# A third factoring level across pairs of octs in a dilated causal convolution, with bank sums by DVE adds and the first ten tiles by the plain tap sum

## The chip, the core and the metric

The kernel runs on one core of one Trainium2 chip. The time is the device time of one execution in microseconds (us), quoted as the median of several executions. A program on one core has no second die to compare with, so "fast" in the run lists means within 1.5% of the fastest run of the same kernel; all runs quoted here are fast. Engines: PE is TensorE (matmuls), PEld its weight loads, DVE is VectorE, ACT is ScalarE, POOL is GpSimd, SP is SyncE, whose queue issues most of the loads here. "ACTq" and "SPq" are the instruction queues of ACT and SP when they issue transfers. In this kernel every matmul writes into one tensor of eight "banks" (0 to 7) in PSUM; all other tiles lie in SBUF. The "granted clock" is the share of full speed at which TensorE ran.

## The reference

```python
# x (2, 16000, 144), w (15, 144, 288), w_o (144, 144), all bf16; dil = 2, K = 15
xp = jnp.pad(x, ((0, 0), (28, 0), (0, 0)))
h = sum over i of einsum('btc,cd->btd', xp[:, 28 - 2*i : 28 - 2*i + T, :], w[i])
f, g = h[..., :144], h[..., 144:]
z = jnp.tanh(f) * _sigmoid(g)
return z @ w_o
```

The 32000 rows are cut into 128 segments of 250 consecutive steps, one segment per partition. "Tile" k holds step k of all segments: 128 rows. Dilation 2 means that tile k needs tiles k, k-2, ..., k-28, so even and odd tiles never meet. Eight consecutive tiles are an "oct": four tiles of each parity. There are 31 octs and 2 tiles ahead of them (called oct -1).

A channel vector of 144 is 128 + 16. The 16 left-over channels of eight taps are packed into one 128-row operand (XB), so a plain tap sum costs 15 + 2 = 17 matmuls of 288 columns per tile.

## The kernel before

A fast-FIR factoring in two levels works on the four tiles of one parity in one oct (a "quad", with parity r). It needs nine short sub-filters, fed with sums of weights (WC, WS) and differences of inputs (VE, VF, DU, DE, DF, BE, BF), instead of 16 pieces of the plain sum: 41 matmuls for four tiles instead of 68.

```python
        def S1(n):                       # 4 matmuls, then a copy of the bank
            o, r = quads[n]
            b = take()
            a = b + 1
            g.add("pe", region(a, [(lambda o_=o - i: XA[:, aslot(o_), r, :]) for i in range(4)], [wc(0, i) for i in range(4)], True), ...)
            g.add("act", lambda e: e.activation(bank(b), bank(a), ACT.Copy), r=[("bank", a)], w=[("bank", b)], dur=0.43)
        # ... S2: VE x 4 into bank a, ACT copies it to U, VF x 4 into bank b, DVE makes DD = bank b - U
        # ... S3: DU x 4 + XB into a and into b, DVE makes two new banks: a + DD, b - DD
        # ... S4: DE / DF / BE / BF products, 19 matmuls, into the four banks; tanh and gate of each pair
```

Per oct: 82 convolution matmuls of 288 columns, then a projection by w_o (11 matmuls of up to 288 columns), for which a transposing load turns z around. All operations are entered into a graph. On the host, a model of the engines (with assumed durations) decides the order in which each engine issues them. That order is then fixed: on the chip an engine waits at its next instruction even if a later one is ready.

```python
SEM_LAT = 0.07
DMA_LAT = 1.9
DMA_RATE = 200e3
MM = 0.12
# ...
            if op.dma:
                free[op.eng] = st + op.dur
                t0 = max(dma_free, st + op.dur)
                dma_free = t0 + op.nbytes / DMA_RATE
                op.end = dma_free + DMA_LAT
```

The inputs of an oct are first copied by DVE into a staging buffer, then loaded, transposed, by SP. There are two staging buffers of each kind, so the copy for oct o waits for the load of oct o-2:

```python
        def load_xb(o):
            s, q = bslot(o), o % NST     # NST = 2
            # ...
            g.add("dve", cp, r=sorted(ck, key=str), w=[("STB", q)], dur=0.36)
            g.add("sp", lambda e: e.dma_start_transpose(XB[:, s, :, :], STB[:, q, :, :].rearrange("p a b -> p (a b)")),
                  r=[("STB", q)], w=[("XB", s)], dur=1.3, dma="xb", nbytes=8 * 128 * 128 * 2)
```

Transfers take turns on a few semaphores. Where there are fewer semaphores than transfers, an issue waits until the earlier transfer on the same semaphore has landed. The raw weights WA come in four pieces, issued by ACT, on three semaphores (`"wa": 3`).

## Time and profile before

| | before |
|---|---|
| median | 379.54 us (379.22 to 380.3, 4 runs) |
| span of the profiled execution | 377.9 us |
| convolution matmuls | 31 x 82 + 34 = 2576 |
| steady state, one oct | 11.03 us |

The page of the kernel before: busy time of each engine with its share of the span, the row of the granted TensorE clock in 40 slices, and the chain of waits by engine.

```profile
PE 364.5 (96%) x3067; PEld 290.3 (77%) x3067; DVE 242.2 (64%) x642; ACT 174.2 (46%) x361; POOL 15.0 (4%) x30
PEclk9999999999999999999999999999999999999996
PE 91%; DVE 5%; DMA 1%; ACT 1%; ACTq 1%; issue 0%
```

The chain of waits follows the work back from the last instruction, at each step to what it had waited for. It is 91% PE: TensorE bounds this kernel. The busy share alone wouldn't have told it. The Trainium skill ("Perfetto Trace Analysis", section "Identifying the Most-Contended Engine") warns that the busy share of matmuls is a poor measure of how close a kernel is to its limit, because matmuls are pipelined. This case agrees, if weakly: PE shows 96% before and after the change, though by the count explained in the result it lost 18.8 us of 378 (5.0%) before and 23.9 us of 369 (6.5%) after.

The chain of waits of the kernel before in one stretch of the steady state (start, length, engine and line):

```profile
223.93 0.25 PE PS L653 x3
224.18 9.55 PE PS L555 x78
233.74 0.74 PE PS L653 x8
234.48 0.49 PE PS L555 x4
234.97 0.25 PE PS L653 x3
```

L555 is a convolution matmul and L653 a projection. One oct is 78 + 4 convolution and 11 projection matmuls, and repeats after 234.97 - 223.93 = 11.04 us. A convolution matmul takes 9.55 / 78 = 0.1224 us. The Trainium skill ("TensorE: Matmul & The Clock Gate", section "Wait — 56ns, not 53.3ns?") gives columns / 2.4 GHz + about 2.5 ns, 122.5 ns for 288 columns, and the trace agrees. So PE has no slack in the steady state; only fewer matmuls can shorten it.

The table by windows of the kernel before (window, length, then busy us and count of PE, PEld, DVE, ACT, POOL, then the clock, the DMA share and GB/s):

```profile
0.00:40.00 40.00, 29.93 (x267) 23.46 (x268) 26.59 (x81) 12.90 (x26) 15.04 (x30) 0.96 0.86 210
40.00:70.00 30.00, 30.00 (x253) 24.11 (x251) 26.24 (x73) 13.12 (x28) 0.00 (x0) 1.00 0.93 206
100.00:200.00 100.00, 100.00 (x845) 80.38 (x844) 67.03 (x175) 48.33 (x100) 0.00 (x0) 1.00 0.58 123
```

PE is full from 40 us on. DVE (67%) and ACT (48%) have room. The start is the weak part: waits of PE there, in the table of PE waits of the kernel before (line that waited, what it waited for: us in total, times, longest):

```profile
PE PS L555 <- DVE DD L689: 2.4, 1, 2.4
PE PS L555 <- DVE XA L419: 2.2, 1, 2.2
```

Together they are 4.6 us in which PE waited for DVE: for the difference DD of two banks (L689) and for an evacuation of transposed x (L419). Both lie in the first 40 us.

### The profile page before, as it was taken

The page shows a single profiled execution, that of the slowest core. Times are in us where ns is not written, and L with a number is a line of the kernel's source. Part 1 is how long each engine was busy: PE and PEld are TensorE (multiplying, and loading weights), DVE is VectorE, ACT ScalarE, POOL GpSimd, SP SyncE. Part 2 cuts the span into 40 slices and gives each one's busy share as a digit, 9 for nine tenths or more (in the row PEclk, how much of TensorE's full clock was granted, in tenths as well). Part 3 has the DMA queues.
Part 4 walks back from the last instruction along what each step waited for, and adds up shares of the span by engine and source line. Part 5 has one row for each costly group of instructions (what it writes and reads, how often), then busy time and mean ns, then how long its engine had stood idle before and what let it go on. Part 6 is the DMA issues. An engine that isn't in the chain of part 4 may idle for free.

```text
span 377.9 us, 7552 instructions
## 1 busy us (share of the span) xinstructions
PE 364.5 (96%) x3067; PEld 290.3 (77%) x3067; DVE 242.2 (64%) x642; ACT 174.2 (46%) x361; POOL 15.0 (4%) x30
## 2 busy tenths in 40 slices
PE   8668999999999999999999999999999999999996
PEld 7445788887888788888788888878888888888873
DVE  1897889777676766677666666766665665553341
ACT  1522454454544445444444544444454444445443
POOL 5820000000000000000000000000000000000000
PEclk9999999999999999999999999999999999999996
DMA  8589969995586644844755356456335434211221
GB/s 224 122 264 243 259 91 264 169 213 134 114 157 182 120 89 93 212 88 94 117 119 94 88 117 88 94 116 121 91 88 120 87 65 91 63 51 44 64 46 49
DMA packets 111647, 46.73 MB, mean 124 GB/s; under 512 B 103598, under 2 KB 106079, under 8 KB 110845
## 3 DMA queue, kind: packets, MB, share of 16 engines
q1 hardware_dynamic: 108858, 44.67, 54.2%
q10 hardware_dynamic: 2243, 1.25, 1.3%
q8 instruction: 24, 0.39, 0.5%
q0 software_dynamic: 512, 0.33, 0.4%
q14 instruction: 10, 0.08, 0.1%
HBM read 11.82 MB, written 9.22 MB: 56 GB/s over the span
## 4 chain that ended last, share of the span: by engine, by line
PE 91%; DVE 5%; DMA 1%; ACT 1%; ACTq 1%; issue 0%
PE PS L555 81%; PE PS L653 8%; DMA WA<-in_w_dram 1%; DVE WC L452 1%; DVE VE L501 1%; PE PS L618 0%; PE PS L620 0%; DVE VF L501 0%; DVE DU L501 0%; DVE DE L501 0%; ACTq L353 0%; DVE STA L472 0%; PE PS L609 0%; DVE WS L452 0%; PE PS L608 0%
## 5 line engine op out<-in xcount | busy, mean ns | idle before, releaser
L584 ACT ACTIVATE TS<-PS 128x576 bf16<-128x576 f32 x125 | 81.5, 652 | 102.1 <-PE PS L555 101.9
L588 DVE SCALAR_TENSOR_TENSOR Z<-TS 128x288 bf16<-128x288 bf16 x125 | 56.9, 455 | 46.6 <-ACT TS L584 46.2
L555 PE MATMUL PS<-WA,DE 128*128 128x288 bf16 x496 | 81.6, 287 | 0.8 <-DVE PS L700 0.8
L555 PE MATMUL PS<-WS,DU 128*128 128x288 bf16 x434 | 71.0, 286 | 2.4 <-DVE DD L689 2.4
L555 PE MATMUL PS<-WA,DF 128*128 128x288 bf16 x434 | 71.2, 286 | 0.2 <-DVE PS L703 0.2
L686 ACT ACTIVATE U<-PS 128x288 f32<-128x288 f32 x62 | 25.5, 411 | 72.6 <-PE PS L555 72.5
L555 PEld LDWEIGHTS PS<-WA,DE 128*128 128x128 bf16 x496 | 47.8, 98 | 13.1 <-DVE PS L700 1.1
L555 PEld LDWEIGHTS PS<-WS,DU 128*128 128x128 bf16 x434 | 42.3, 98 | 13.3 <-DVE DD L689 2.7
L555 PEld LDWEIGHTS PS<-WA,DF 128*128 128x128 bf16 x434 | 42.2, 98 | 11.2 <-DVE PS L703 0.6
L689 DVE TENSOR_TENSOR DD<-PS,U 128x288 f32<-128x288 f32 x62 | 28.3, 457 | 30.6 <-PE PS L555 20.6
L658 ACT ACTIVATE OS<-PS 128x432 bf16<-128x432 f32 (+1 forms) x91 | 41.2, 488 | 13.9 <-PE PS L653 13.6
L555 PE MATMUL PS<-WC,VE 128*128 128x288 bf16 x248 | 41.0, 289 | 0.7 <-ACT PS L676 0.5
L555 PE MATMUL PS<-WC,XA 128*128 128x288 bf16 x248 | 40.5, 286 | 0.4 <-DVE WC L452 0.4
L653 PE MATMUL PS<-WOR,ZT 128*128 128x144 bf16 (+1 forms) x333 | 39.8, 253 | 0.0
L555 PE MATMUL PS<-WB,XB 128*128 128x288 bf16 x128 | 36.2, 286 | 0.0
L555 PE MATMUL PS<-WB,BE 128*128 128x288 bf16 x124 | 35.6, 287 | 0.0
L555 PE MATMUL PS<-WB,BF 128*128 128x288 bf16 x124 | 35.5, 286 | 0.0
L501 DVE TENSOR_TENSOR BF<-XB 128x512 bf16<-128x512 bf16 x31 | 13.1, 423 | 34.1 <-PE PS L555 34.1
L555 PE MATMUL PS<-WC,VF 128*128 128x288 bf16 x186 | 33.3, 289 | 0.0
L653 PEld LDWEIGHTS PS<-WOR,ZT 128*128 128x128 bf16 x333 | 27.8, 98 | 5.8
L703 DVE TENSOR_TENSOR PS<-PS,DD 128x288 f32<-128x288 f32 x62 | 28.6, 462 | 5.2 <-PE PS L555 0.9
L555 PEld LDWEIGHTS PS<-WC,VE 128*128 128x128 bf16 x248 | 24.1, 98 | 7.3 <-ACT PS L676 0.8
(71 smaller groups left out, 366.0 us busy)
## 6 DMA issues: line engine op xcount, KB each, us to landing
out_dram<-OS SPq DMA_DIRECT2D x30, 288.0 KB, 2.2
Xr<-in_x_dram SPq DMA_DIRECT2D x6, 1152.0 KB, 6.2
WA<-in_w_dram ACTq DMA_DIRECT2D x3, 288.0 KB, 7.2
Xr<-in_x_dram SPq DMA_DIRECT2D x1, 864.0 KB, 4.5
Xr<-in_x_dram SPq DMA_DIRECT2D x2, 288.0 KB, 5.2
Xr<-in_x_dram SPq DMA_DIRECT2D x1, 576.0 KB, 4.5
Xp<-in_x_dram SPq DMA_DIRECT2D x2, 252.0 KB, 5.4
XA<-STA SPq DMA_TRANSPOSE x31, 3.3
```

What stands on the lines that cost most here:

```text
L452: g.add(eng, lambda v: v.tensor_tensor(dst(), a(), b(), ALU.add), r=r, w=wk, dur=dur)
L501: return g.add("dve", lambda v: v.tensor_tensor(dst(), a(), b(), ALU.subtract), r=r, w=wk, dur=dur)
L555: return lambda t: t.matmul(bank(b), lhsT=lhs(), rhs=rhs(), start=start, stop=True, skip_group_check=True)
L584: return a.activation(TS[:, s, :, :], src, ACT.Tanh)
L588: return v.scalar_tensor_tensor(dst, TS[:, s, :, D:N2], 1.0, TS[:, s, :, 0:D], ALU.add, ALU.mult)
L653: return t.matmul(PS[:, c0:c0 + n * D], lhsT=ZT[:, zt, blk_, :], rhs=WOR[:, wi_:wi_ + n, :].rearrange("p a b -> p (a b)"), start=first, st ...
L658: return a_.activation(OS[:, os_, a0:c0, :].rearrange("p e d -> p (e d)"), PS[:, bo * 512:bo * 512 + (c0 - a0) * D], ACT.Copy, scale=0.5)
L686: g.add("act", lambda e: e.activation(U[:, u, :], bank(a), ACT.Copy), r=[("bank", a)], w=[("U", u)], dur=0.43)
L689: g.add("dve", lambda v: v.tensor_tensor(DD[:, u, :], bank(b), U[:, u, :], ALU.subtract), r=[("bank", b), ("U", u)], w=[("DD", u)], dur=0.48)
L703: g.add("dve", lambda v: v.tensor_tensor(bank(e), bank(b), DD[:, u, :], ALU.subtract), r=[("bank", b), ("DD", u)], w=[("bank", e)], dur=0.48)
```

## The change

Its intent: fewer matmuls in the steady state, and a start in which PE has useful work while DVE makes the weight sums and differences.

- Two successive octs (30 octs make 15 pairs) share three of the nine sub-filters. For such a sub-filter, two octs need 2 common products and 2 difference products each, instead of 4 each: 6 instead of 8. A "unit" is one parity of one pair, 8 tiles: 76 matmuls (2x2 XC, 2x6 XR, 2 SC, 2x2 SR, 2x8 EF, 2x19 DD) instead of 82.
- The sums of banks that put the sub-filters together are four DVE adds per half unit, PSUM + SBUF into PSUM. ACT copies more banks: bank 7 to 6, p to q, p to p+1, and both X banks to SBUF (UX).
- Oct 0 and the two tiles of oct -1 (10 tiles) go by the plain tap sum: 170 matmuls, which need only transposed x and raw weights.
- The projections are no longer placed where they fit; they stand in PE's main order and use banks 6 and 7 by turns.
- The host's model is new: other durations, a latency per engine, priorities; `DMA_RATE` 300e3 instead of 200e3. `DMA_LAT` stays 1.9 us.

```diff
-SEM_LAT = 0.07
+SEM_LAT = 0.05
 DMA_LAT = 1.9
-DMA_RATE = 200e3
-MM = 0.12
+DMA_RATE = 300e3
+MM = 0.122
+LAT = {"pe": 0.17, "act": 0.12, "dve": 0.08, "pool": 0.1, "sp": 0.0}
 # ... the scheduler uses LAT and a priority
+        def common(b, t0, t1, i0, keys):
+            g.add("pe", [mm(b, t0, lambda: WT[:, i0, :], True), mm(b, t1, lambda: WT[:, i0 + 1, :], False)], ...)
+        def XC(u, k):          # 2 products common to both octs, bank 7, ACT copies it to bank 6
+        def XR(u, k):          # 2 + 1 products for each oct into banks 7 and 6, ACT takes both to UX
+        def SC(u):             # 2 common products into bank p, ACT copies p to q
+        def SR(u, h):          # 2 products for oct h, ACT copies p to p+1
+        def EF(u, h):
+            # ... 4 VE products into p, 4 VF products into p + 1
+            for dst, src, k in ((n, p, 0), (n + 1, p + 1, 0), (p, p, 1), (p + 1, p + 1, 1)):
+                g.add("dve", lambda v, dst=dst, src=src, k=k: v.tensor_tensor(bank(dst), bank(src), UX[:, k, us, h, :], ALU.add), ..., prio=0)
+        # ... DD: the 19 products of S4, as before
+        for u in range(NUN):
+            def slot(b):
+                if todo:
+                    project(*todo.pop(0), b)
+            EF(u, 0)
+            slot(6)
+            # ... XC, DD, XR of this and the next unit
+            if u == NUN - 1:
+                ship_pair(o1, 6, -2, BANK_O)
+                ship_pair(o1, 2, -2, BANK_O)
+                store_some(o1, [2, 6], 2, 4, 0)
+            slot(7)
+            EF(u, 1)
+            slot(6)
+            # ...
```

`ship_pair` is the way out of the last oct: PE transposes z, DVE and ACT evacuate, PE projects, ACT evacuates. It stood in the kernel before too; new is that its two early calls stand in front of `slot(7)`, `EF(u, 1)` and `slot(6)`. `slot(b)` places the next waiting projection, in bank b, so these projections use the same banks 6 and 7 as the early calls.

> **What bounds it now.** TensorE. The chain of waits is 91% PE, 81% of it convolution matmuls. In steady state it repeats every 11.03 us per oct (8 output tiles): 82 matmuls of 288 columns in 10.04 us, 122.4 ns each, plus 11 projection matmuls in 0.99 us. The Trainium skill ("TensorE: Matmul & The Clock Gate", section "Wait — 56ns, not 53.3ns?") gives columns/2.4 GHz + 2.5 ns back to back, 122.5 ns here: the trace agrees. The table by windows shows PE 100% busy from 40 to 370 us, DVE 67%, ACT 48%. In the first 40 us PE does roughly 12 us of useful work; the chain runs through DVE from 10.9 to 26 us (weight sums, differences), and in part until 37. The tail after the last convolution matmul is 8.8 us.
>
> **PE work.** For 8 tiles 82 matmuls become 76: each of three shared sub-filters takes 2 common + 2x2 difference products for two octs instead of 8. 30 units: 180 less. Oct 0 goes by plain tap sum: 10 tiles x 17 = 170 matmuls instead of 34 + 82 = 116, 54 more. Net -126 x 0.1224 = **-15.4 us**. Projections are unchanged.
>
> **The start.** Plain tap sums need only transposed x and raw weights, so PE works 20.8 us (170 x 0.1224) while DVE makes sums and differences. Before, tap sums began at 15.1 us; I expect 13 to 15.5, ending at 34 to 36. DVE has about 24 us of work (0.34 us per difference back to back, 0.31 to 0.38 per sum) from 11 us on, done near 35. The first unit then pays a serial run matmul, ACT copy, matmul, evacuation: 3 us. PE's steady run starts near 38 us with oct 0 done; before, oct 0 was in its last phase at 37. Worth another 5 to 8 us.
>
> **DVE and ACT.** Per 8 tiles DVE does 8 PSUM adds (0.37 us apart) instead of 6, plus 0.5 us of second-level differences: 8.3 to 9 us of 10.3, over 80%. ACT does five copies (0.41) and two double evacuations (0.65) instead of four copies: 7.3 of 10.3, 71%. Neither becomes the bound, but both now stand in short loops: matmul, copy of bank 7 to 6, matmul, evacuation, with the projection sharing those banks; and matmuls, four adds, matmuls. Timing one unit by hand leaves slack of 0.2 to 0.5 us at most steps, nearly none where the shared bank's copy must precede the next products. I allow 0.1 us per unit, 3 us in all; it could be 10.
>
> **Sum** (span): 36 (start) + 3 (first unit) + 30 x 76 x 0.1224 = 279.1 + 30 x 0.99 = 29.7 + 3 (stalls) + about 8 (tail) = 358.8; time was 1.8 us above the span: **360 us**, range 354 to 368. Faster by over 2% (below 372): 0.92; within: 0.06; slower: 0.02.
>
> **What would show it.** In the chain, an oct pair every 20.6 us (22.06 before); convolution matmuls about 2450; PE nearly 100% busy from 40 us on; PE waits for ACT copies or DVE adds under 5 us; tap sums filling 14 to 35 us with no DVE chain there; DVE over 80%, ACT near 70%. If the pair takes over 21.3 us, the short loops stall PE and the gain halves; the table of PE waits will name adds or copies.
>
> **What would make it wrong.** In-order DVE at 80% load delaying adds behind differences; the projection's eviction holding banks 6 and 7; a first unit waiting for the transposing loads of octs 1 and 2, now issued only after the weights have landed.

## The result, and the profile after

| | before | after |
|---|---|---|
| median | 379.54 us (379.22 to 380.3, 4 runs) | 370.02 us (369.66 to 371.04, 4 runs) |
| ratio after / before | | 0.9751, 95% interval 0.9726 to 0.9775 |
| span of the profiled execution | 377.9 us | 369.3 us |
| convolution matmuls | 2576 | 2450 |
| steady state, 8 tiles | 11.03 us | 10.30 us |

A ratio is the mean time of one kernel's fast runs over that of the other's fast runs of the same rounds, so it isn't quite the ratio of the medians. The kernel is faster by 2.5%, as the direction said, but 370 us lies above the predicted 354 to 368 us.

The page of the kernel after, the same three lines, and the chain by line:

```profile
PE 353.4 (96%) x2971; PEld 279.7 (76%) x2971; DVE 266.6 (72%) x729; ACT 225.4 (61%) x449; POOL 18.5 (5%) x30
PEclk9999999999999999999999999999999999999978
PE 78%; DMA 11%; DVE 7%; ACT 1%; SPq 1%; issue 1%; ACTq 1%
PE PS L588 69%; PE PS L690 7%; DMA XB<-STB 7%; DMA WA<-in_w_dram 2%; DMA Xr<-in_x_dram 1%; DVE STB L506 1%; DMA XA<-STA 1%; DVE Z L621 1%; DVE WC L468 1%; SPq L508 1%; DVE PS L767 1%; DVE VE L517 0%; DVE BF L517 0%; PE PS L651 0%; ACTq L366 0%
```

The chain was 91% PE and is now 78% PE: 11% of the span is spent in loads, 7% of it in the transposing load of XB. The clock row has two slices below 9 at its end.

The chain of waits of the kernel after in the steady state:

```profile
84.59 5.02 PE PS L588 x41
89.61 0.37 PE PS L690 x4
89.98 3.31 PE PS L588 x27
93.29 0.37 PE PS L690 x4
93.66 0.98 PE PS L588 x8
94.64 0.25 PE PS L690 x3
94.89 5.02 PE PS L588 x41
```

41 + 27 + 8 = 76 convolution and 11 projection matmuls in 94.89 - 84.59 = 10.30 us for 8 tiles, 20.60 for a pair of octs. That is the predicted number exactly. The table by windows of the kernel after:

```profile
0.00:40.00 40.00, 34.69 (x330) 28.81 (x330) 25.73 (x82) 10.92 (x21) 18.46 (x30) 0.96 0.89 204
40.00:70.00 30.00, 25.17 (x203) 18.95 (x204) 26.79 (x76) 16.54 (x35) 0.00 (x0) 1.00 1.05 225
100.00:200.00 100.00, 99.45 (x840) 79.32 (x839) 80.57 (x221) 67.58 (x134) 0.00 (x0) 1.00 0.64 135
```

In the steady state all is as predicted: PE 99%, DVE 81%, ACT 68%. PE does more in the first 40 us (34.69 us busy instead of 29.93). But from 40 to 70 us PE is busy 25.17 us of 30, and before it was full there. So the missing gain isn't in the steady state. It is in the first pairs and at the ends.

To put sizes to this, I counted the time that PE lost: for each two successive matmuls of the trace, the distance of their starts less columns / 2.4 GHz + 2.5 ns. Half clock counts as lost. This is my sum over the trace's records, not a view of the profile.

| stretch | lost before | lost after |
|---|---|---|
| 0 to 39.3 us (after: until the last tap sum) | 14.1 | 8.0 |
| 39.3 to 70 us | 0 | 6.0 |
| 70 to 349 us | 0 | 1.7 |
| 349 us to the last matmul | 4.7 (all after 363) | 8.2 |
| all | 18.8 | 23.9 |

The start gained 6.1 us and gave 6.0 of it back in the first pairs. The end lost 3.5 us more than before. What is left is the smaller PE work: the span less the lost time fell from 359.1 to 345.4 us, by 13.7 us. The prediction had 15.4 us for the convolution matmuls alone; the new start also has 16 more transposes and 16 more warm-up matmuls of 128 columns, an estimated 1.8 us by the same formula (32 x 0.056), less two of 288 columns.

**The first pairs.** The table of PE waits of the kernel after:

```profile
PE PS L588 <- DVE PS L767: 4.4, 5, 1.4
```

L767 are the DVE adds of banks. PE waited for them only five times in 60 half units, up to 1.4 us each, and the three longest of these lie before 70 us (at 46.77, 53.38 and 63.94 us). It isn't a little in every unit. Why were the adds late? The timeline of DVE in the kernel after, around the second of these waits (start, length, engine, line, operation, tiles, shape, count, then in brackets the idle time before it and what ended it):

```profile
49.89 0.43 DVE L506 COPY STB<-XBc 128x1024 bf16<-128x1024 bf16 x1 [1.26 <-DMA XB<-STB]
...
51.25 0.43 DVE L488 COPY STA<-Xr 128x1024 bf16<-128x1024 bf16 x1 [0.22 <-DMA XA<-STA]
...
52.86 1.55 DVE L767 TENSOR_TENSOR PS<-PS,UX 128x288 f32<-128x288 f32 x4
```

and the timeline of PE in the same kernel:

```profile
51.56 0.41 PE L588 MATMUL PS<-WT,DU 128*128 128x288 bf16 x2
53.38 0.66 PE L588 MATMUL PS<-WA,DE 128*128 128x288 bf16 x4 [1.41 <-DVE PS L767]
```

DVE stood idle for 1.26 us at the copy into a staging buffer whose earlier load hadn't landed, and 0.22 us at the next. The adds stood behind these copies in DVE's order and were late by about as much as PE waited: 1.41 us. Before the first of the three waits DVE had stood 3.3 us for loads, 2.08 us of it at one staging copy at 28.06 us; before the third, 0.89 us. The Trainium skill ("Perfetto Trace Analysis", section "Tensor Engine Instruction (MATMUL, LD_WEIGHTS)") calls DVE and ACT strict first-in, first-out; the trace agrees: DVE idles at the copy and runs nothing from behind it.

The chain of waits of the kernel after shows the same loads in its first part:

```profile
21.80 6.23 DMA XB<-STB
...
47.84 3.38 DMA XA<-STA
...
57.80 4.93 DMA XB<-STB
```

The host's model gives such a transposing load 1.9 us + 262144 bytes / 300e3 = 2.8 us. In these lines it took 3.4 to 6.2 us; all those issued in the first 40 us of this trace took 2.5 to 6.2 us, 4.3 us in the median. The Trainium skill ("DMA: Bandwidth & Descriptors", section "Anatomy of one DMA — SWDGE (gpsimd) path") fits 2.0 us + bytes / 436e3 to transfers issued by GpSimd, 2.6 us for this size as an estimate: these loads, issued by SP among many others, are slower than that, and the measured times decide.

**The start.** The timeline of ACT in the kernel after:

```profile
2.75 6.56 ACTq L356 DMA_DIRECT2D WA<-in_w_dram  x2
...
11.00 1.02 ACT L423 ACTIVATE XA<-PS 128x1024 bf16<-128x1024 bf16 x1 [8.09 <-issue]
```

ACT is held 6.56 us at the issue of weight pieces: the fourth must wait for the semaphore of the first. Only at 11.00 us does ACT evacuate its first transposed x, and the first tap sum starts at 16.58 us.

**The end.** The timeline of PE in the kernel after, inside the last unit:

```profile
352.47 0.23 PE L651 MATMUL PS<-WOR,ZTL 128*128 128x144 bf16 x1 [0.47 <-ACT ZTL L645]
...
353.70 0.23 PE L641 MATMUL PS<-ID,Z 128*128 128x128 bf16 x1 [0.50 <-ACT OS L656]
...
356.36 0.90 PE L690 MATMUL PS<-WOR,ZT 128*128 128x144 bf16 x4 [0.50 <-ACT OS L656]
357.05 1.17 PE L588 MATMUL PS<-WC,VE 128*128 128x288 bf16 x4
```

Two `ship_pair` calls one after the other, each a chain PE, ACT, PE, ACT, through the banks that the next projection in PE's order needs. PE must wait for all of it. Four waits of about 0.5 us (the third of them, at 354.88, is left out above) are 1.9 us; but the four products at 357.05 then show 1.17 us, where a group of four has 0.65 us elsewhere. The table by windows of the kernel after, around it:

```profile
351.30:354.90 3.60, 2.15 (x15) 1.04 (x12) 1.20 (x4) 1.69 (x4) 0.00 (x0) 0.98 0.30 56
356.40:361.60 5.20, 5.20 (x24) 3.43 (x25) 1.66 (x4) 0.94 (x2) 0.00 (x0) 0.50 0.24 75
```

The granted clock is 0.50 for that stretch; the trace's clock records put it at half from 354.78 to 361.61 us. The Trainium skill ("TensorE: Matmul & The Clock Gate", section "What's actually happening") speaks of a free-running window of 3413 ns and of half clock after an idle window. The length agrees: 6.83 us is two windows, and in four other profiles (after_again, wa_sem4, ring4, lat4) the clock is at half for one, 3.41 us, at this place. But the window before the fall wasn't idle: PE was busy 2.15 us of 3.60, and no wait was over 0.50 us. The same page (section "A second HAM failure mode: psum-queue depth-cycling") does tell of many short idles between groups of matmuls that bring the clock down; that is nearer to what is seen here.

### The profile page after: what moved, and what is told of

Same layout as the page of the kernel before. It is cut to its first block, busy times and chain, and to the rows that moved or that the text cites. A ratio compares the mean times of both kernels' runs of the same rounds, so it can differ in the third digit from the quotient of the medians.

```text
span 369.3 us, 7518 instructions
## 1 busy us (share of the span) xinstructions
PE 353.4 (96%) x2971; PEld 279.7 (76%) x2971; DVE 266.6 (72%) x729; ACT 225.4 (61%) x449; POOL 18.5 (5%) x30
## 4 chain that ended last, share of the span: by engine, by line
PE 78%; DMA 11%; DVE 7%; ACT 1%; SPq 1%; issue 1%; ACTq 1%
PE PS L588 69%; PE PS L690 7%; DMA XB<-STB 7%; DMA WA<-in_w_dram 2%; DMA Xr<-in_x_dram 1%; DVE STB L506 1%; DMA XA<-STA 1%; DVE Z L621 1%; DVE WC L468 1%; SPq L508 1%; DVE PS L767 1%; DVE VE L517 0%; DVE BF L517 0%; PE PS L651 0%; ACTq L366 0%
## 5 line engine op out<-in xcount | busy, mean ns | idle before, releaser
L767 DVE TENSOR_TENSOR PS<-PS,UX 128x288 f32<-128x288 f32 x240 | 94.4, 458 | 4.2 <-PE PS L588 4.0
L588 PE MATMUL PS<-WA,DE 128*128 128x288 bf16 x480 | 79.0, 288 | 4.5 <-DVE PS L767 4.4
L694 ACT ACTIVATE OS<-PS 128x432 bf16<-128x432 f32 (+1 forms) x91 | 44.3, 488 | 36.8 <-PE PS L690 36.8
L716 ACT ACTIVATE PS<-PS 128x288 f32<-128x288 f32 x150 | 59.3, 397 | 9.7 <-PE PS L588 7.0
L690 PE MATMUL PS<-WOR,ZT 128*128 128x144 bf16 (+1 forms) x333 | 45.2, 256 | 0.5 <-ACT OS L656 0.5
L588 PE MATMUL PS<-WS,GU 128*128 128x288 bf16 x210 | 44.1, 286 | 0.7 <-ACT PS L716 0.7
L737 ACT ACTIVATE UX<-PS 128x576 f32<-128x576 f32 x60 | 38.9, 648 | 3.9 <-PE PS L588 1.4
L588 PEld LDWEIGHTS PS<-WS,GU 128*128 128x128 bf16 x210 | 20.5, 98 | 6.4 <-ACT PS L716 1.2
L588 PE MATMUL PS<-WT,DU 128*128 128x288 bf16 x120 | 24.5, 286 | 0.7 <-ACT UX L737 0.7
L588 PE MATMUL PS<-WC,GX 128*128 128x288 bf16 x120 | 24.3, 286 | 0.0
```

The lines of the kernel that those rows point to most:

```text
L588: return lambda t: t.matmul(bank(b), lhsT=lhs(), rhs=rhs(), start=start, stop=True, skip_group_check=True)
L690: return t.matmul(PS[:, c0:c0 + n * D], lhsT=ZT[:, zt, blk_, :], rhs=WOR[:, wi_:wi_ + n, :].rearrange("p a b -> p (a b)"), start=first, st ...
L694: g.add("act", lambda e: e.activation(OS[:, os_, a:c, :].rearrange("p e d -> p (e d)"), PS[:, bo * 512:bo * 512 + (c - a) * D], ACT.Copy, ...
L716: g.add("act", lambda e: e.activation(bank(c), bank(b), ACT.Copy), r=[("bank", b)], w=[("bank", c)], dur=0.29, prio=prio)
L737: return e.activation(UX[:, k, u % NU, :, :], src, ACT.Copy)
L767: g.add("dve", lambda v, dst=dst, src=src, k=k: v.tensor_tensor(bank(dst), bank(src), UX[:, k, us, h, :], ALU.add), r=[("bank", src), ("UX ...
```

## The experiments

The theory: the change does what it should in the steady state, and the prediction's miss is three separate things, each at a place of its own: (a) the two output pairs in PE's order in the last unit, with the half clock they bring on; (b) ACT's queue held by a missing semaphore in the start; (c) DVE adds in the first pairs, behind copies that wait for loads, because the order was made with too short a load latency.

Rivals: the end is only the clock, or only the waits; (c) is a shortage of staging buffers, not a wrong order; the short loops of copies and adds stall PE in every unit; and the whole gain is the better model of the scheduler, not the factoring.

All kernels of this section give the right result. Times are medians of four executions, five for the last one; every call had its own runs of the kernel before on the same chip (medians 378.78, 377.80, 379.63 and 378.15 us in the four calls). tail_moved, tail_warm, wa_sem4 and ring4 ran together; then after_again, ringAB, best1 and best2; then lat4, best3 and before_sched; then best5. They are told here by what they test.

### tail_moved: the two output pairs later in PE's order, through another bank

```diff
-            if u == NUN - 1:
-                ship_pair(o1, 6, -2, BANK_O)
-                ship_pair(o1, 2, -2, BANK_O)
-                store_some(o1, [2, 6], 2, 4, 0)
             slot(7)
             EF(u, 1)
             slot(6)
+            if u == NUN - 1:
+                ship_pair(o1, 6, -2, UB[u][0])
+                ship_pair(o1, 2, -2, UB[u][0])
+                store_some(o1, [2, 6], 2, 4, 0)
```

> The changed kernel with the last oct's two early output pairs moved behind the second half of the last unit, and their transposes put into a bank pair that is free by then, so that no projection waits for them. Theory (order of banks 6 and 7 stalls PE, and the idle lowers the granted clock): the 5.95 us lost on PE from 350 to 360 us and most of the 2.3 us after it go, the granted clock stays near full until the last few us, and the time falls from 370 by 4.5 to 6.5 us. Rival (this tail is work and latency that any order pays: the output transposes, copies and stores of the last oct): the time stays within 1.5 us of 370.

Measured: 364.06 us (363.11 to 366.25), ratio to before 0.9620 (0.9575 to 0.9665). This interval lies below that of the unedited kernel in the repeat further down (0.9678 to 0.9774). From 349 us to the last matmul PE lost 3.7 us instead of 8.2, and from the start of the last unit to the last instruction it took 17.4 us instead of 21.9. The clock didn't fall in this stretch, and the first four products of `EF(u, 1)` took 0.65 us instead of 1.17, in PE's timeline of tail_moved:

```profile
351.40 0.65 PE L588 MATMUL PS<-WC,VE 128*128 128x288 bf16 x4
```

So the waits and the half clock both came from the pairs as they stood. This is (a). The edit changed the place of the pairs and the banks of their transposes together; whether one of the two would have been enough wasn't tested.

### tail_warm: keep the waits, give PE dummy work in them

```diff
             if u == NUN - 1:
                 ship_pair(o1, 6, -2, BANK_O)
                 ship_pair(o1, 2, -2, BANK_O)
                 store_some(o1, [2, 6], 2, 4, 0)
+                for _ in range(22):
+                    g.add("pe", lambda t: t.matmul(PS[:, UB[u][0] * 512:UB[u][0] * 512 + N2], lhsT=ID[:], rhs=WARM[:], start=True, stop=True, skip_group_check=True),
+                          r=["ID", "WARM"], w=[("bank", UB[u][0])], dur=MM)
```

> The changed kernel with 22 dummy matmuls put between the steps of the stalled tail, so that PE waits as before but is not idle. It prices the clock part alone. If the lower granted clock after the stall costs what the matmul spacing says (240 instead of 122 ns for some 22 matmuls), the time falls by 1.5 to 3 us, while the waits for the output copies keep their place; if the clock is not lowered by this idle, the time stays or rises by up to 0.5 us.

Measured: 367.73 us (366.29 to 369.85), ratio 0.9713 (0.9667 to 0.9759). This interval overlaps that of the unedited kernel (0.9678 to 0.9774 in the repeat below), so the times alone don't decide it. The traces do: from the start of the last unit to the end 19.9 us instead of 21.9 (20.7 in the repeat), and the group of four at full speed again, in PE's timeline of tail_warm:

```profile
356.10 0.65 PE L588 MATMUL PS<-WC,VE 128*128 128x288 bf16 x4
```

Idling for the pairs thus has two costs: the waits themselves and the half clock behind them. All profiles of this study bear this out. In the six with the pairs in their old place and no dummy matmuls the clock fell to half in the last unit: twice for 6.83 us (after, ringAB: 21.9 and 21.7 us from the start of the last unit to the end) and four times for 3.41 us (20.6 to 20.8 us). tail_warm has no such fall (19.9 us), nor have the five with the pairs moved (17.4 to 17.6 us). So the half clock cost 0.7 to 2.0 us and the waits 2.3 to 2.6 us. Neither rival ("only the clock", "only the waits") holds.

### wa_sem4: one more semaphore for the weight pieces

```diff
-        g.assign(mksem, {"xp": 8, "wa": 3, "wb": 2, "xr": NX, "xa": 4, "xb": 6, "zt": 3, "st": 4, "wor": 16})
+        g.assign(mksem, {"xp": 8, "wa": 4, "wb": 2, "xr": NX, "xa": 4, "xb": 6, "zt": 3, "st": 4, "wor": 16})
```

> The changed kernel with four instead of three semaphores for the four weight loads, so that the ACT queue no longer waits for the first load to land before it issues the last one; same order on every engine. Theory (ACT begins its evacuations at 11.0 us because its queue is held by that wait): ACT starts by about 8.5 to 9.5 us, the first tap-sum matmul moves from 16.6 to about 14 to 15.5 us, the end of the tap sums moves with it, and the time falls by 1 to 2.5 us. Rival (the landing of the weights and of x sets the start): first tap-sum matmul within 0.5 us of 16.6 and the time within 0.7 us of 370.

Measured: 366.41 us (365.24 to 368.57), ratio 0.9693 (0.9646 to 0.9740); again the intervals overlap, and the trace decides. ACT's timeline in wa_sem4:

```profile
2.76 1.10 ACTq L356 DMA_DIRECT2D WA<-in_w_dram  x2
...
7.48 1.02 ACT L423 ACTIVATE XA<-PS 128x1024 bf16<-128x1024 bf16 x1 [4.56 <-PE PS L415]
```

The issue takes 1.10 us instead of 6.56, ACT starts at 7.48 us instead of 11.00, and what it waited for until then was PE's transposes, its real input. Tap sums begin at 13.63 us, a little earlier than expected, and the first unit at 34.71 us (39.33 without the edit). Over all profiles of this study, tap sums begin at 15.2 to 17.0 us in the seven profiles of the new kernel without this edit (17.0 us in after_again) and at 13.5 to 13.9 us in the five with it. This is (b). Of the 4.6 us at the end of the tap sums 2.9 are the earlier beginning; the other 1.7 are the half clock from 16.86 us on, which wa_sem4 doesn't have. None of the five profiles with this edit has it in the tap sums, and five of the seven without it do; why isn't shown. The first EF starts at 40.44 us instead of 43.93: part of the 4.6 us is lost again, because PE now waits 1.8 us for DVE's differences across the two octs (GU) in the first unit. The waits for adds are still there, 3.0 us in all.

### ring4: four staging buffers for STB, with the order kept

```diff
-    NST = 2
+    NST, NSB = 2, 4
-        STB = sb("STB", [NP, NST, 8, 128], BF16)
+        STB = sb("STB", [NP, NSB, 8, 128], BF16)
 # ... in load_xb; ring_dma[o] is the load of oct o
-            s, q = bslot(o), o % NST
+            s, q = bslot(o), o % NSB
-            g.add("dve", cp, r=sorted(ck, key=str), w=[("STB", q)], dur=0.34)
+            cop = g.add("dve", cp, r=sorted(ck, key=str), w=[("STB", q)], dur=0.34); held.append((cop, ring_dma.get(o - 2)))
 # ...
-        _ms = g.schedule()
+        held = [(c, d) for c, d in held if d is not None and d not in c.deps]; [c.deps.add(d) for c, d in held]; g.schedule(); [c.deps.discard(d) for c, d in held]
```

The copy's old dependence on the load of oct o-2 is put back while the host makes the order and dropped after it, so that the order is the same on every engine and only the wait is gone; the copy still waits for the load of oct o-4 from its own slot.

> The changed kernel with four instead of two staging buffers in front of the transposing loads of the narrow channel block; same order on every engine, only that wait is gone. Theory (in-order DVE stands behind a staging copy that waits for a transposing load of two octs before, and the adds that PE needs stand behind it): the 5.8 us that DVE waits for that load go, the PE waits for the adds fall from 4.4 to under 1.5 us, and the time falls by 2.5 to 4.5 us. Rival (DVE simply has too much to do in the first pair, waits or not): the PE waits for the adds stay above 3 us and the time within 1 us of 370.

Measured: 366.54 us (365.84 to 368.57), ratio 0.9686 (0.9645 to 0.9727). PE's waits and DVE's waits in the kernel ring4 (two answers, PE first):

```profile
PE PS L588 <- DVE PS L767: 2.7, 2, 1.4
```

```profile
DVE STA L488 <- DMA XA<-STA: 4.1, 7, 1.8
```

This interval, too, overlaps that of the unedited kernel. Behind the second of PE's waits for adds, up to 300 us, the loss went from 2.7 us (1.7 in the repeat) to 0.6 us. But the first two waits stayed, and DVE now waits at the other kind of copy, STA, for 4.1 us (0.7 before). The expectation held in part: DVE's waits for the narrow block's loads are gone, but PE's waits for adds fell only to 2.7 us, not under 1.5.

### after_again and ringAB: the repeat, and four staging buffers of both kinds

after_again is the kernel after, unedited, so that the second call has its own reference. ringAB gives STA four slots too, with the same order on every engine. The two extra slots of each kind lie in Xp, a buffer of x that is dead by then; their copies wait for its last readers.

```diff
-    NST = 2
+    NST, NSB = 2, 4
 # ... in load_xa and load_xb: o % NSB; slots 2 and 3 are in Xp
-            s, q = aslot(o), o % NST
+            s, q = aslot(o), o % NSB
 # ... dependences on the load of oct o-2 held for the order only, as in ring4
```

> The changed kernel unchanged, on the same chip as the next ones, to compare them on one chip: 0.975 of the kernel before. The spread of its start is of interest: if the landing of the first weights varies from run to run, the first tap-sum matmul will not be at 16.6 us again, but between 15 and 17.

> The changed kernel with four staging buffers for both transposing loads (two of each in the space of the x block that only the start uses); same order on every engine. ring4, with four for the narrow block only, took away all losses after 60 us but left two waits for adds of 1.5 us near 43 and 50 us. Theory (those two are the same thing on the wide block: DVE waited 1.8 us at 49 for a staging buffer of it): the wait at 50 us goes, waits for adds fall to under 1.8 us in all, and the time is 0.5 to 2 us below ring4's ratio of 0.9686. Rival (in the first pair DVE is simply behind with the preparations, which stand before the adds in its order): both waits stay at over 1 us each and the time equals ring4's.

Measured: after_again 368.26 us (366.20 to 369.17), ratio 0.9726 (0.9678 to 0.9774); ringAB 366.09 us (365.99 to 366.78), ratio 0.9675 (0.9636 to 0.9714). In ringAB nothing is lost after 70 us, but PE still waits 2.5 us for adds in the first pairs. DVE's waits in ringAB:

```profile
DVE XBc L386 <- DMA Xr<-in_x_dram: 3.9, 2, 2.5
```

With no staging buffer to wait for, DVE waits at the next thing in its order, the chunk of x itself. The expectation was missed, and the time equals ring4's within the intervals, as the rival said. That spoke against "too few buffers" as the cause of the first waits: here buffers more moved the wait to the next load in the order.

### lat4: the load latency of the host's model, alone

```diff
-DMA_LAT = 1.9
+DMA_LAT = 4.0
```

Two staging buffers as in the change; only the order in which the engines issue differs. PE's order is the same; DVE's and that of the loads on SP are not, and on ACT one evacuation moves. One clause of the expectation, on the latency of early loads, is cut, because the traces don't show its range; what the trace of the change shows is stated above (2.5 to 6.2 us).

> The changed kernel with one constant of the host's scheduling model changed: the latency that it takes for a load, 4.0 instead of 1.9 us (the traces show 3.3 us for a transposing load[...]). PE's order stays, DVE's static order changes: copies that wait for loads move behind other work. Theory (the adds stand behind waiting copies because the model that made the order takes loads to be faster than they are): DVE's waits for loads fall from about 6 us to under 3, PE's waits for adds from 3 to 4.4 us to under 2, ratio 0.965 to 0.970 against 0.9726 to 0.9751 of the changed kernel. Rival (only the number of buffers matters): the waits and the time stay, 0.972 to 0.976.

Measured: 365.50 us (363.41 to 366.79), ratio 0.9642 (0.9618 to 0.9666), below the interval of after_again (on another chip, each against the kernel before on its own). The table of PE waits no longer names the adds, and DVE's waits for loads are 0.4 us in all. PE's timeline in lat4, at the place shown above:

```profile
48.33 0.41 PE L588 MATMUL PS<-WT,DU 128*128 128x288 bf16 x2
48.57 0.65 PE L588 MATMUL PS<-WA,DE 128*128 128x288 bf16 x4
```

The 1.41 us in front of the second group are gone. From the end of its tap sums (37.8 us) to 340 us PE lost 2.6 us, where the change unedited lost 7.5 us from 39.3 to 340, and 5.8 us in the repeat; 1.4 of the 2.6 are the serial first unit. This is (c): the cause was the order, made for loads of 2.8 us (whether DVE's or that of the loads on SP isn't separated). With another order two buffers were enough, while four buffers in the old order left the first waits.

### before_sched: the kernel before with only the new model of the scheduler

```diff
-SEM_LAT = 0.07
+SEM_LAT = 0.05
-DMA_RATE = 200e3
-MM = 0.12
+DMA_RATE = 300e3
+MM = 0.122
+LAT = {"pe": 0.17, "act": 0.12, "dve": 0.08, "pool": 0.1, "sp": 0.0}
 # ... and the priorities and durations of the change
```

> The kernel before with the other half of the change alone: the new host model (latencies, priorities, durations) without the third level, the plain tap sums and the new buffers. Theory (the gain is fewer matmuls): PE was already dense from 40 us on, so at most the 14 us lost in the first 40 us can move; ratio 0.990 to 1.005. Rival (a good part of the change's 2.5% is better scheduling): 0.985 or below.

Measured: 382.56 us (382.38 to 384.34), ratio to before 1.0090 (1.0064 to 1.0117). The new model alone makes the old kernel slower by 0.9%, a little beyond the expected 0.990 to 1.005. So the gain is the factoring and the start by tap sums, with the order of work that goes with them, and the rival falls. Neither of the two was run without the other; their shares come from the count above alone (13.7 us less PE work; 6.1 us won in the start, of which 6.0 were lost again).

### best1, best2, best3: mends put together, with the larger staging rings

best1 is tail_moved + wa_sem4 + ringAB. best2 is best1 with the differences DU of both octs, and the second-level differences made from them, ahead of the others in DVE's preparation. best3 is tail_moved + wa_sem4 + lat4 with the larger rings known to the model.

```diff
 # best2, against best1
         def prepare(m):
-            prep(2 * m + 1)
-            prep(2 * m + 2)
+            v_second(2 * m + 1)
+            v_second(2 * m + 2)
+            for o in (2 * m + 1, 2 * m + 2):
+                v_first(o)
+                v_third(o)
+                b_diffs(o)
 # best3, against best1
-DMA_LAT = 1.9
+DMA_LAT = 4.0
 # ... and no dependences held for the order: the model sees four slots
```

> The three mends together: tail pairs moved, four weight semaphores, four staging buffers of both kinds. If the three are independent losses, their gains add: about 5 + 2 to 3 + 2.5 us, ratio 0.945 to 0.952 of the kernel before, which is 358 to 361 us at this kernel's 379 and what the prediction said of the change. If they hide one another (an earlier start only makes DVE wait for its loads), 0.955 to 0.96.

> best1 with the preparation of a pair in another order: the second-level differences, which the first matmuls of a pair need, before the others. In all runs so far PE waited 0.8 to 1.9 us for them in front of the first unit. Expected: that wait under 0.5 us, time 0.5 to 1.5 us below best1; if DVE's total work up to the first adds is the limit, the wait only moves to the adds and the time is that of best1 within 0.7 us.

> best1 (0.9565) with the same constant, and with the model told of the four buffers. In best1 PE lost 2.2 us at 40.6 us and then ran at a low clock until 46, behind a copy that waited for a chunk of x. Expected: that loss under 1 us, 1 to 3 us less than best1, ratio 0.949 to 0.954. If the load itself is the limit (its issue comes late on the queue), it stays at 0.956.

Measured: best1 361.78 us (361.18 to 362.89), ratio 0.9565 (0.9528 to 0.9603); best2 362.32 us (361.88 to 363.01), ratio 0.9578 (0.9543 to 0.9613); best3 366.30 us (365.96 to 366.93), ratio 0.9653 (0.9635 to 0.9672). All three missed the gain that was hoped for. best1 and best2 fell where the alternative in their expectations had put them (0.955 to 0.96; within 0.7 us of best1); best3 was worse than both branches of its expectation.

In best1 DVE reached the chunk of x early and stood there, ahead of the adds. The timeline of DVE in best1:

```profile
38.77 0.23 DVE L386 COPY XBc<-Xr 128x256 bf16<-128x256 bf16 x1 [1.73 <-DMA Xr<-in_x_dram]
```

PE then waited 2.2 us in all for adds, and the clock records show half clock from 43.5 to 46.9 us after it. In best2 PE waited for adds 3.9 us in all, 2.8 us at the longest: the wait only moved. In best3, PE's waits name something new:

```profile
PE PS L690 <- DMA ZT<-Z: 5.5, 2, 2.7
```

With large rings in the model, copies and loads are issued far ahead, and the transposing load of z, which the projection needs, stands behind them in SP's queue. So a larger ring with a good latency was worse than a small ring with a good latency. That the loads issued early cause this wait is argued from their order in the queue; best5, with small rings, tests it.

### best5: the three mends with the two staging buffers of the change

```diff
-DMA_LAT = 1.9
+DMA_LAT = 4.0
 # ... the two output pairs moved as in tail_moved
-        g.assign(mksem, {"xp": 8, "wa": 3, ...})
+        g.assign(mksem, {"xp": 8, "wa": 4, ...})
```

> The changed kernel with three mends: tail pairs moved, four weight semaphores, load latency of 4.0 us in the model, and the two staging buffers as they were. best3 waited 5.5 us for the transposing load of the output, which stood on the load queue behind the loads that four buffers let it issue early; lat4, with two buffers, waited 0.4 us for it. If that is the reason, the gains of the three mends add: about 1.2% (tail) + 0.5% (weights) + 0.9% (model) below the changed kernel's 0.974, ratio 0.944 to 0.951, and the wait for the output's load stays under 1 us. If an earlier start alone brings it back, ratio 0.955 or above.

Measured: 358.40 us (357.53 to 359.99, five runs), ratio to before 0.9491 (0.9466 to 0.9516). The expectation (0.944 to 0.951) held: PE's waits for the load of z are 0.8 us in all. best5 is faster than both kernels. Its page:

```profile
PE 348.4 (98%) x2971; PEld 277.8 (78%) x2971; DVE 266.2 (75%) x729; ACT 226.0 (64%) x449; POOL 18.1 (5%) x30
PEclk9999999999999999999999999999999999999999
PE 89%; DMA 4%; DVE 3%; ACT 2%; SPq 1%; issue 0%
```

The table by windows of best5, at the place where the change had 25.17:

```profile
40.00:70.00 30.00, 29.33 (x245) 22.94 (x243) 28.11 (x80) 19.26 (x38) 0.00 (x0) 1.00 1.03 219
```

The chain is 89% PE again, the clock is full until 1 us before the end, and PE is busy 29.33 us of 30 from 40 to 70 us with no wait for adds. PE lost 10.4 us in all: 4.8 in the first 39.3 us, 1.6 from there to 340 us, and 3.9 at the end.

| kernel | edit | median us | ratio to before, with interval | place of the effect |
|---|---|---|---|---|
| after_again | none | 368.26 | 0.9726 (0.9678 to 0.9774) | |
| tail_moved | pairs later | 364.06 | 0.9620 (0.9575 to 0.9665) | end |
| tail_warm | dummy matmuls | 367.73 | 0.9713 (0.9667 to 0.9759) | end, clock only |
| wa_sem4 | 4 semaphores | 366.41 | 0.9693 (0.9646 to 0.9740) | start |
| ring4 | 4 STB buffers | 366.54 | 0.9686 (0.9645 to 0.9727) | waits after the first two |
| ringAB | 4 + 4 buffers | 366.09 | 0.9675 (0.9636 to 0.9714) | the wait moves on |
| lat4 | latency 4.0 us in the model | 365.50 | 0.9642 (0.9618 to 0.9666) | first pairs |
| before_sched | new model, old kernel | 382.56 | 1.0090 (1.0064 to 1.0117) | |
| best5 | three mends | 358.40 | 0.9491 (0.9466 to 0.9516) | all three |

## Why the prediction was right or wrong

The prediction was a sum for the span. Its terms against the traces of the change and of best5:

| term | predicted | after | best5 |
|---|---|---|---|
| tap sums end | 36 | 39.3 | 34.6 |
| PE work of 30 units (279.1 + 29.7) | 308.8 | 309.1 | 308.8 taken |
| first unit, and stalls of all units | 3 + 3 | 7.7 | 4.5 |
| lost inside the last unit | 0 | 6.7 | in the line above |
| after the last convolution matmul | 8 | 6.5 | 7.9 |
| span | 358.8 | 369.3 | 355.8 |

For the change, the PE work is 362.85 (end of the last convolution matmul) - 39.3 less 7.7 + 6.7 lost. For best5 the predicted work is taken as given, and the 4.5 us are what remains of 347.9 - 34.6; they hold the early output pairs, too.

- **What bounds it, and the steady state: right.** A pair of octs in 20.6 us was predicted and measured; convolution matmuls about 2450, measured 2450; DVE over 80%, measured 80.6%; ACT near 70%, measured 67.6%. The short loops of copies and adds hardly stall PE in the steady state (1.7 us from 70 to 349 us). The waits for adds and ACT copies, which were to stay under 5 us, were 5.8 us (4.4 and 1.4), most of them before 70 us.
- **"an oct pair every 20.6 us ... PE nearly 100% busy from 40 us on": the second half is wrong.** PE was busy 25.17 us of the 30 from 40 us on.
- **"The start": the step failed by 3.3 us.** "I expect 13 to 15.5, ending at 34 to 36": it was 16.58 and 39.3. The prediction took ACT's evacuations of x for granted and didn't see that ACT's queue is held by the fourth weight piece (wa_sem4 began at 13.63 us). The rest, 1.7 us, is clock: in the profiled run it was at half from 16.86 to 20.28 us, so that the first 90 matmuls of the tap sums took 12.7 us instead of 11.0. Its "roughly 12 us of useful work" in the first 40 us of the kernel before was too low as well: the trace has 138 convolution matmuls there, an estimated 16.9 us at 0.1224.
- **"I allow 0.1 us per unit, 3 us in all": wrong in kind and in place.** With 3 us for the first unit, the term was 6 us and measured 7.7, so the size was off by little. But it isn't a little in each unit: 6.0 of the 7.7 us lie before 70 us, and from there to 349 us the units lost 1.7 us together. Among what would make it wrong, the prediction named "In-order DVE at 80% load delaying adds behind differences" and "a first unit waiting for the transposing loads". Both happened, joined in one: adds behind copies that wait for loads. lat4 took it away.
- **"about 8 (tail)": the step that failed most.** After the last convolution matmul it was 6.5 us, less than predicted. But the prediction began its tail there and had nothing for the last unit itself, in which 6.7 us were lost to the two early output pairs and the half clock that they brought on. tail_moved showed the cause, and tail_warm and the other profiles put 0.7 to 2.0 us of it down to the clock alone. The prediction had named "the projection's eviction holding banks 6 and 7" among what would make it wrong, but for the loop as a whole: in the last unit PE did wait for ACT's evictions (two of the four waits, 1.0 us). It gives no term for the special case of the main loop at the last unit.
- **The confidence** of 0.92 for over 2% was borne out only just: 2.5%. The three misses had one sign, and the range of 354 to 368 allowed for stalls, not for faults at both ends together.

The sum was nearer to what the change can do than to what it did: with the three faults mended, 358.4 us against the predicted 360. That agreement is partly luck, since best5's start ended earlier than predicted and its stalls were fewer, and since the kernel before ran at 378.15 us beside best5 and at 379.54 us in the result.

What stays open: why the first weights land between 7.0 and 9.3 us in different profiles; why best1 and best3 fall behind best5 in full detail; whether the last unit's pairs had to change their place, their banks or both; and the 10.4 us that best5 still loses, of which 4.8 are in the start.

## What to carry to other kernels

When a change makes the steady state of a full engine shorter, work out the two ends and the first few rounds as carefully as the steady state: here nearly all of the 10 us by which the prediction missed lay in the first 70 and the last 20 us. Where a host fixes the order of in-order engines, give its model the latencies that the trace shows under load; here another buffer only moved the first waits to the next load in the same order. And don't put a latency chain that passes through a shared bank in front of the main engine's work: here it cost 2.3 to 2.6 us in waits and then 0.7 to 2.0 us by the clock.

## What the Trainium skill lacked or had wrong

- "TensorE: Matmul & The Clock Gate", section "What's actually happening": half clock is put down to an idle window of about 3.4 us. Here the clock fell to half at 354.78 us after a window in which PE was 60% busy (2.15 of 3.60 us, longest wait 0.50 us), and stayed for 6.83 us. The clock fell before the last convolution matmul in all six profiles with the pairs at this place and no dummy matmuls, and in none of the six others of the new kernel. The page's section on psum-queue depth-cycling names short idles as a cause, but no busy share at which they count.
- "DMA: Bandwidth & Descriptors", section "Anatomy of one DMA — SWDGE (gpsimd) path": the fit of about 2.0 us + bytes / 436e3 is for transfers issued by GpSimd and would give an estimated 2.6 us for 256 KB. A transposing load of that size issued from SP took 3.3 us in the median, and up to 7.0 us in the first 60 us. The section "Latency and other measured facts" gives a bandwidth for transposing loads (261 GB/s with a non-contiguous middle dimension), but no time from issue to landing.
- The same page, section "Issuing engines are not separate DMA queues": the time that initiating a transfer takes of the sequencer is called usually small against the transfer. Here the 91 transposing loads of one execution held SP's queue for 1.33 us in the median (1.24 to 3.43 us), against 3.3 us to their landing.
- No page was found that has the spacing of back-to-back DVE adds from PSUM into PSUM (the table of cycle counts in "VectorE: DVE Perf Modes" has results in SBUF only): a 128x288 f32 add (PSUM + SBUF into PSUM) is recorded as 0.46 us long, but four of them take 1.55 us, so one follows another after 0.36 to 0.37 us.
